# Loading v in the layout in which its products read it, and smaller edits around it

## The chip, the cores and the metric

The kernel runs on one core of a Trainium2 chip. The core has five engines with an instruction stream each: TensorE (PE) for matrix products into the accumulator memory (PSUM), VectorE (DVE), ScalarE (ACT) and GpSimd (POOL) for element-wise work, and SyncE (SP), which here only starts transfers. Sixteen DMA engines move data between the chip's memory and the core's working memory (SBUF, 128 partitions). The metric is the device time of one execution, in microseconds.

## The reference, cut to what matters

Two stages follow each other. The first is an attention without a softmax: each row of q and k (4 batches, 4 heads, 1088 tokens of 32 numbers) is sketched to two vectors of 8 numbers, and their outer product has 64 features. The second adds to the result the real part of its two-dimensional Fourier transform, normalizes each row and applies a small network of two layers.

```python
def phi(x):
    a = np.einsum('rd,bhsd->bhsr', S1, x)
    b = np.einsum('rd,bhsd->bhsr', S2, x)
    return np.einsum('bhsi,bhsj->bhsij', a, b).reshape(*x.shape[:-1], r * r)
q_p, k_p = (phi(q), phi(k))
kv = np.einsum('bhsf,bhsd->bhfd', k_p, v)
z = np.sum(k_p, axis=2)
num = np.einsum('bhsf,bhfd->bhsd', q_p, kv)
den = np.einsum('bhsf,bhf->bhs', q_p, z)[..., None] + 1e-06
x = num / den                        # then heads side by side: (4, 1088, 128)

X = np.fft.fft(np.fft.fft(x, axis=1), axis=2)
u = x + np.real(X)
un = (u - u.mean(-1)) / np.sqrt(u.var(-1) + 1e-06)
out = u + np.maximum(un @ w_ch1, 0.0) @ w_ch2
```

The sum z is a product with a column of ones, so the kernel appends ones to v and gets kv and z from one product.

## The kernel before, in words

The program is a list of named steps (`add` in `program`). Their order is written out by hand in `ORDER`, and with it the order of the instructions on each engine; each engine works its own list strictly in that order and waits where an input is not there yet. Where a step may run on several engines, `ENGINE` names one, else the first allowed is taken. `BANK` names the PSUM banks of each step, so a step also waits until the last reader of its bank is done. The token `11@0` in `ORDER` stands for eleven products of zeros into bank 0: they have no result and keep PE busy.

The batches are worked in the order 1, 0, 3, 2. The 1088 tokens of a head are 64 groups of 17. For one batch:

- **Loads** (SP): `ld_k`, `ld_v`, `ld_q`, each one transfer of 544 KB to 128 partitions. The tiles k_in, v_in and q_in have three buffers each, so the fourth batch's load waits until the third buffer has been read. The order on SP is k1, k0, q0, v1, q1, k3, v0, q3, w1, v2, w2, k2, v3, q2.
- **Features of k**: `kT` (DVE) transposes k in blocks of 32, `kproj` (PE) multiplies it by the sketches for all four heads at once (`sblk`), `kab` (ACT or DVE) copies the result out of PSUM, and four `kp` steps (POOL or DVE) form the outer products. The 16 tokens of a group that fill whole tiles take this way; `kproj` puts token 2t + h of each group in tile t, partitions 64 h and up. The seventeenth token has its own steps: `kt_pr`, `kt_a`, `kt_p`.
- **v**: `vcopy` (steps `vc`, on ACT or POOL) brings v into that token order and next to a column of ones (tile `v`, 33 of 36 columns), `vlast` (`vl`) does so for the seventeenth token (tile `vt`). The ones are written once (`c_v1`, `c_vt`).
- **Sums**: `kv` (PE, L396) multiplies the outer products by v and its ones, 33 columns, over 8 tiles and the seventeenth token (`kvt`); `kvz` copies the sums to where the next product reads them.
- **Features of q**: `qT`, `qt_T` (DVE transposes), `qfeat` (PE), `qa` (ACT copy out of PSUM), `qp` (DVE product); `pnd` (PE, L496) multiplies them by the sums, `den` and `xx` (DVE) divide.
- **Transform and network**: foldings of x by POOL and DVE, `srow` (PE), copies `zev`, `zrev`, `zleft` (steps `z`, `zr`, `zl`), then ten mixer units with `mix` or, for the seventeenth tokens of two batches, `mixl` (PE), row statistics, a transpose, the two layers, the copy `fin` and the store.

The start of the program also computes tables of sines and cosines (`t_` and `d_` steps) and constants (`c_` steps, mostly on POOL). The sketches S1 and S2 arrive by ACT's transfers `ld_s` and are transposed by PE in `s_t`; `s_blk` (DVE) makes `sblk` of it.

PE writes each 32-bit product as two records, so that the 36 products of `kv` per batch are 72 records.

## Time and profile before

| | |
|---|---|
| median of 3 runs | 82.59 us (82.38 to 83.35) |
| profiled execution | 82.68 us, of which span 80.9 us |
| PE, DVE busy | 70.3 us (87%), 65.8 us (81%) |
| ACT, POOL busy | 57.3 us (71%), 48.5 us (60%) |
| DMA queue of SP | 5332 packets, 9.31 MB |
| granted TensorE clock | 0.978 |

The span runs from the first to the last instruction of the profiled execution; the other 1.8 us of its time lie around it. Busy time is what an engine spent in instructions that compute; a share near one says that the engine is full, not that it is what the others wait for. The rows of a timeline give start and length in microseconds, engine, line, operation, output and inputs with their shapes, the number of instructions merged into the row, and in brackets how long the engine stood idle before it and who released it. Rows of busy times by stage give the stretch, its length, then busy time and count of PE, PE's weight loads, DVE, ACT and POOL, the granted clock, the share of time in which the DMA engines were busy, and GB/s.

### The profile page before, as it was taken

How to read it: one execution, taken by the hardware profiler on the slowest of the kernel's cores; microseconds unless marked ns; L12 is line 12 of the kernel's file. 1: busy time of each engine (PE TensorE's matmuls, PEld its weight loads, DVE VectorE, ACT ScalarE, POOL GpSimd, SP SyncE). 2: the span in 40 equal slices, each digit the busy share in tenths (PEclk: the TensorE clock that was granted, in tenths of full speed). 3: DMA queues.
4: the chain of work that ended last, by engine and by line, in shares of the span. 5: the costliest groups of instructions: out<-in, count | busy, mean ns of one | idle time of the engine just before them, and what ended most of it. 6: DMA issues, size and time to landing. Idle time of an engine off the chain costs nothing.

```text
span 80.9 us, 3298 instructions
## 1 busy us (share of the span) xinstructions
PE 70.3 (87%) x1380; PEld 51.7 (64%) x1385; DVE 65.8 (81%) x142; ACT 57.3 (71%) x106; POOL 48.5 (60%) x130
## 2 busy tenths in 40 slices
PE   4999997999999999999697999979999898999000
PEld 1326944969799887559576795655866793578000
DVE  2999839999989999999998959997987799867300
ACT  1447679999999996858619686785779889695100
POOL 6898699999799996879999990952400000000000
PEclk9999999999999999999999999999999999999965
DMA  1899999970360700000000000000035440404450
GB/s 23 300 424 409 420 420 392 373 263 23 39 245 17 271 0 4 8 0 0 8 0 8 0 0 0 8 0 0 0 91 169 128 139 12 135 15 138 116 161 14
DMA packets 5570, 9.65 MB, mean 119 GB/s; under 512 B 564, under 2 KB 3380, under 8 KB 5556
## 3 DMA queue, kind: packets, MB, share of 16 engines
q1 hardware_dynamic: 5332, 9.31, 33.4%
q8 instruction: 11, 0.18, 0.9%
q10 hardware_dynamic: 224, 0.14, 0.6%
q14 instruction: 3, 0.02, 0.1%
HBM read 7.22 MB, written 2.23 MB: 117 GB/s over the span
## 4 chain that ended last, share of the span: by engine, by line
PE 50%; POOL 24%; DVE 8%; ACT 7%; issue 3%; DVEq 1%; POOLq 0%; ACTq 0%
PE ps L496 8%; PE ps L673 7%; PE ps L396 7%; PE ps L651 6%; PE ps L444 6%; POOL t_kp__129 L79 4%; POOL t_kp__132 L79 3%; PE ps L560 3%; POOL t_kp__133 L79 3%; PE ps L591 2%; PE ps L643 2%; DVE t_x__147 L506 2%; PE ps L566 2%; POOL t_ph L185 2%; POOL t_e__149 L79 2%
## 5 line engine op out<-in xcount | busy, mean ns | idle before, releaser
L813 PE MATMUL ps<-t_wz 128*128 128x512 bf16 x19 | 6.8, 519 | 1.3 <-DVE t_eps L127 1.2
L72 ACT COPY t_qa__139<-ps 128x1024 f32<-128x1024 f32 x4 | 4.0, 1012 | 2.8 <-PE ps L444 2.8
L666 ACT ACTIVATE t_ht__112<-ps 128x1024 bf16<-128x1024 f32 x4 | 4.1, 1024 | 2.0 <-PE ps L651 1.8
L813 PEld LDWEIGHTS <-t_wz 128*128 128x128 bf16 x20 | 2.2, 121 | 4.7 <-issue 2.9
L651 PEld LDWEIGHTS <-t_w1b 128*128 128x128 bf16 x40 | 3.3, 97 | 3.0 <-issue 1.3
L72 ACT COPY t_qa__138<-ps 128x1024 f32<-128x1024 f32 x4 | 4.0, 1009 | 1.5 <-PE ps L444 1.5
L666 ACT ACTIVATE t_ht__111<-ps 128x1024 bf16<-128x1024 f32 (+1 forms) x4 | 3.5, 910 | 0.9 <-PE ps L651 0.7
L666 ACT ACTIVATE t_ht__113<-ps 128x1024 bf16<-128x1024 f32 x4 | 4.0, 1021 | 0.1
L651 PE MATMUL ps<-t_unT__178,t_w1b 128*128 128x512 bf16 (+1 forms) x14 | 3.4, 333 | 0.4 <-DVE t_x__147 L506 0.2
L651 PE MATMUL ps<-t_unT__180,t_w1b 128*128 128x512 bf16 x11 | 3.3, 378 | 0.4 <-ACT t_ht__112 L666 0.2
L454 DVE TENSOR_TENSOR t_qp__141<-ps,t_qa__139 128x1024 f32<-128x1024 f32 x2 | 2.5, 1225 | 1.4 <-ACT t_qa__139 L72 1.2
L496 PE MATMUL ps<-t_kvz,t_qp__140 128*64 128x66 f32 x96 | 3.4, 223 | 0.0
L496 PE MATMUL ps<-t_kvz,t_qp__141 128*64 128x66 f32 x96 | 3.4, 223 | 0.0
L496 PEld LDWEIGHTS ps<-t_kvz,t_qp__140 128*64 128x64 f32 x96 | 3.1, 138 | 0.4 <-ACT t_kvz L72 0.4
L496 PEld LDWEIGHTS ps<-t_kvz,t_qp__141 128*64 128x64 f32 x96 | 3.1, 138 | 0.0
L444 PE MATMUL ps<-t_qT__125,t_sa 32*64 32x256 f32 x64 | 2.9, 400 | 0.0
L444 PE MATMUL ps<-t_qT__126,t_sa 32*64 32x256 f32 x64 | 2.9, 400 | 0.0
L196 ACT ACTIVATE t_pm<-t_ph 128x290 f32<-128x290 f32 x3 | 1.3, 441 | 2.1 <-DVE t_ph L190 2.1
L668 DVE TENSOR_SCALAR t_ht__114<-ps 128x1024 bf16<-128x1024 f32 x2 | 2.4, 1221 | 0.4 <-PE ps L651 0.4
L79 POOL TENSOR_TENSOR t_kp__129<-t_ab__128 128x256 f32<-128x256 f32 x4 | 2.4, 628 | 0.5 <-issue 0.5
L444 PE MATMUL ps<-t_qT__126,t_sb 32*64 32x256 f32 x64 | 2.7, 374 | 0.0
L444 PE MATMUL ps<-t_qT__125,t_sb 32*64 32x256 f32 x64 | 2.7, 374 | 0.0
(338 smaller groups left out, 263.0 us busy)
## 6 DMA issues: line engine op xcount, KB each, us to landing
t_k_in__101<-in_k_dram SPq DMA_DIRECT2D x2, 544.0 KB, 6.4
t_q_in__107<-in_q_dram SPq DMA_DIRECT2D x2, 544.0 KB, 3.3
t_v_in__104<-in_v_dram SPq DMA_DIRECT2D x2, 544.0 KB, 7.4
out_dram<-t_ot__110 SPq DMA_DIRECT2D x6, 128.0 KB, 3.1
out_dram<-t_ot__108 SPq DMA_DIRECT2D x6, 128.0 KB, 2.3
t_k_in__100<-in_k_dram SPq DMA_DIRECT2D x1, 544.0 KB
t_k_in__99<-in_k_dram SPq DMA_DIRECT2D x1, 544.0 KB, 4.8
t_q_in__105<-in_q_dram SPq DMA_DIRECT2D x1, 544.0 KB, 5.6
```

Of the source, the lines that this page charges most:

```text
L72: nc.scalar.copy(out, in_)
L79: (nc.vector if e == "DVE" else nc.gpsimd).tensor_tensor(out=out, in0=in0, in1=in1, op=op)
L396: nc.tensor.matmul(ps(f"kv{b}", 33 * (h // 2), [[1, 33]], 64 * (h % 2), 64), w, v, start=(b, h % 2) not in begun, stop=True, tile_position ...
L444: nc.tensor.matmul(ps(f"q{b}.{w}", 512 * h + 256 * f, [[1, 256]], 64 * v, 64), view(T(src), 0, [[1, F]], 32 * h, 32), view(T(f"qT{b % 2}") ...
L454: nc.vector.tensor_tensor(out=view(T(f"qp{(2 * b + w) % 3}"), 127 * w, [[256, 4], [128, 2], [1 - 2 * w, 128]]), in0=ps(f"q{b}.{w}", 256, [ ...
L496: nc.tensor.matmul(ps(f"nd{b}", 512 * (i // 6) + 66 * (i % 6), [[1, 66]], 64 * h, 64), q, z, start=True, stop=True, tile_position=(0, 64 * ...
L560: nc.tensor.matmul(o, w, row(c, t, trig), start=(t == 0), stop=(t == 2), tile_position=(0, p), skip_group_check=True)
L651: nc.tensor.matmul(ps(use, 128 * n * i, [[1, 128 * n]]), T("w1b")[:, 128 * c:128 * c + 128], T(f"unT{g % 3}")[:, 0:128 * n], start=True, s ...
L666: nc.scalar.activation(out=out, in_=in_, func=ACT.Relu)
L668: nc.vector.tensor_relu(out, in_)
L673: nc.tensor.matmul(ps(u, 128 * t, [[1, 128]]), ht_view(g, 512 * c + 128 * t, [[1, 128]]), T("w2b")[:, c, :], start=False, stop=True, skip_ ...
L813: nc.tensor.matmul(made["ps"][:, at, :], made["wz"][:, 0:128], made["wz"][:], start=True, stop=True)
```

## The change

- `ld_v` loads v as two transfers of 64 partitions, one for each half y: partition 64 y + p gets, for each of the four heads, tokens 8 y to 8 y + 8 of group p, nine rows of 32 numbers in one piece. Token 8 is loaded twice, token 16 lies in the upper half only. v_in has four buffers, and behind the loaded rows each holds 32 ones, written once by `c_v1`.
- `vcopy`, `vlast`, the tiles `v` and `vt`, and `c_vt` are gone. `kv` reads v_in directly, 32 columns of v and the 32 ones as 64 columns; `kvz` reads the first 33 of each 64.
- `kproj` puts token t + 8 h, instead of 2t + h, in tile t, so that the outer products meet v in that order. The seventeenth token's features stand in partitions 64 to 127 for all four heads: `kt_pr` is one product of 64 columns instead of two of 32, and `kt_a` and `kt_p` work on 64 partitions with twice the columns.
- `mixl` adds x by one product with the identity `idb` per batch instead of two with `idl`, whose step `c_idl` is gone; `zleft` writes zl with gaps, so that the last rows come out in natural order, and `st_last` stores 128 rows of equal distance. `c_fz` clears the whole of zl.
- In `ORDER` the zero products around the transpose of the sketches become 13 ahead of it and 1 behind, from 11 and 5. All other steps keep their order.

```diff
     def ld_v(b):
-        nc.sync.dma_start(view(T(f"v_in{min(b, 2)}"), 0, [[TT * D, 2], [1, TT * D]]),
-                          dram(x["v"], b * H * S * D, [[TT * D, 128], [2 * S * D, 2], [1, TT * D]]))
+        for y in range(2):
+            nc.sync.dma_start(view(T(f"v_in{b}"), 0, [[9 * D, H], [1, 9 * D]], 64 * y, 64),
+                              dram(x["v"], (b * H * S + 8 * y) * D, [[TT * D, 64], [S * D, H], [1, 9 * D]]))
...
-        nc.gpsimd.memset(view(T("zl"), 16, [[48, 2 * B], [1, 16]]), 0.0)
+        nc.gpsimd.memset(T("zl")[:], 0.0)
...
+        add(f"c_v1{b}", "POOL DVE", "", f"v1:{b}", lambda e, b=b: (nc.gpsimd if e == "POOL" else nc.vector).memset(T(f"v_in{b}")[:, ONES:ONES + D], 1.0))
...
-                                 view(T(f"kT{b % 2}"), 64 * (2 * t + h), [[1, 64]]),
+                                 view(T(f"kT{b % 2}"), 64 * (t + 8 * h), [[1, 64]]),
...
     def kt_pr(b):
-        for u in range(2):
-            nc.tensor.matmul(ps(f"kt{b}", 0, [[1, 32]], 64 * u, 64), view(T(f"kT{b % 2}"), 64 * (TT - 1), [[1, 64]]),
-                             view(T("sblk"), 16 * u, [[32, 2], [1, 16]]), start=True, stop=True,
-                             tile_position=(0, 64 * u), skip_group_check=True)
+        nc.tensor.matmul(ps(f"kt{b}", 0, [[1, 64]], 64, 64), view(T(f"kT{b % 2}"), 64 * (TT - 1), [[1, 64]]), T("sblk")[:],
+                         start=True, stop=True, tile_position=(0, 64), skip_group_check=True)
...
-    def vcopy(b, y, e):
-
-        for u in range(2):
-            copy(e, view(T(f"v{b % 3}"), VP * u, [[2 * VP, 2], [VP * H, 8], [1, D]], 64 * y, 64),
-                 view(T(f"v_in{min(b, 2)}"), D * y, [[TT * D, 2], [2 * D, 8], [1, D]], 64 * u, 64))
-
-    def vlast(b, e):
-        copy(e, view(T("vt"), 2 * VP * b, [[VP, 2], [1, D]]), view(T(f"v_in{min(b, 2)}"), (TT - 1) * D, [[TT * D, 2], [1, D]]))
...
-                nc.tensor.matmul(ps(f"kv{b}", 33 * (h // 2), [[1, 33]], 64 * (h % 2), 64), w, v,
-                                 start=(b, h % 2) not in begun, stop=True, tile_position=at, skip_group_check=True)
+                nc.tensor.matmul(ps(f"kv{b}", 64 * (h // 2), [[1, 64]], 64 * (h % 2), 64), w,
+                                 view(T(f"v_in{b}"), at, [[ONES - at, 2], [1, D]], p, n),
+                                 start=(b, h % 2) not in begun, stop=True, tile_position=(p, 64 * (h % 2)), skip_group_check=True)
...
     def mixl(i):
         u = f"u{i}.2"
         for b in (2 * i, 2 * i + 1):
-            for par in range(2):
-                p, to = 64 * (b % 2), 64 * par + 32 * (b % 2)
-                nc.tensor.matmul(ps(u, 0, [[1, 128]], to, 32), view(T("idl"), 32 * par, [[1, 32]], p, 64),
-                                 view(T(f"x{b}"), 8 * DM, [[1, DM]], p, 64),
-                                 start=True, stop=False, tile_position=(p, to), skip_group_check=True)
+            p = 64 * (b % 2)
+            nc.tensor.matmul(ps(u, 0, [[1, 128]], p, 64), T("idb")[p:p + 64, p:p + 64], view(T(f"x{b}"), 8 * DM, [[1, DM]], p, 64),
+                             start=True, stop=False, tile_position=(p, p), skip_group_check=True)
...
-c_wz c_bias c_iota c_rows ld_k1.0 t_turn0 c_last c_kvz1 t_ph0 c_mask c_fwd c_v12 c_kvz2 ld_s c_vt c_eye16 kT1.0 11@0
-s_t s_blk 5@1 kt_pr1 ld_k0.0 c_v11 t_turn1 kT0.0 t_pm0 kpr1 t_cos0 s_ab t_sin0 kab1 kt_a1 ld_q0.0 c_tab kpr0 kab0
+c_wz c_bias c_iota c_rows ld_k1.0 t_turn0 c_last c_kvz1 t_ph0 c_mask c_fwd c_v12 c_v13 c_kvz2 ld_s c_eye16 kT1.0 13@0
+s_t s_blk 1@1 kt_pr1 ld_k0.0 c_v11 t_turn1 kT0.0 t_pm0 kpr1 t_cos0 s_ab t_sin0 kab1 kt_a1 ld_q0.0 c_tab kpr0 kab0
```

## The prediction

> **What bounds the kernel now.** I read the page's busy times first, then the engines by stage, then the timelines of TensorE (PE) and VectorE (DVE), then the loads. The page:

> ```profile
> span 80.9 us, 3298 instructions
> PE 70.3 (87%) x1380; PEld 51.7 (64%) x1385; DVE 65.8 (81%) x142; ACT 57.3 (71%) x106; POOL 48.5 (60%) x130
> ```

> No engine is idle for long, so the answer lies in stages. The busy times by stage:

> ```profile
> core 0: us, PE busy (x) PEld busy (x) DVE busy (x) ACT busy (x) POOL busy (x), PEclk, DMA share, GB/s
> 18.10:39.30 21.20, 21.20 (x604) 17.93 (x604) 20.05 (x35) 18.54 (x39) 18.87 (x49) 1.00 0.19 59
> ```

> From 18.1 to 39.3 us PE has no gap at all and DVE is busy for 20.05 of 21.2 us. The copies of v are on ACT and POOL; in this stage they are bystanders unless PE or DVE wait for them. The chain of work hands the time before 18.1 us to POOL:

> ```profile
> 16.45 1.67 POOL t_kp__129 L79 x2
> 18.11 2.86 PE ps L396 x88
> ```

> That reading is coarse: the first L396 products after 18.1 us read other tiles, and t_kp__129 comes last of batch 0's. So I go by the timelines. DVE:

> ```profile
> 11.76 1.23 DVE L454 TENSOR_TENSOR t_qp__141<-ps,t_qa__139 128x1024 f32<-128x1024 f32 x1 [1.24 <-ACT t_qa__139 L72]
> ...
> 14.80 0.25 DVE L368 TENSOR_TENSOR t_ktp__123<-ps,t_kta__121 128x128 f32<-128x128 f32 x1
> 15.21 1.22 DVE L454 TENSOR_TENSOR t_qp__140<-ps,t_qa__138 128x1024 f32<-128x1024 f32 x1 [0.15 <-ACT t_qa__138 L72]
> 16.35 0.23 DVE L461 STREAM_TRANSPOSE t_qtT__116<-t_q_in__107 128x64 f32<-128x64 f32 x1
> ...
> 17.54 0.41 DVE L472 TENSOR_TENSOR t_qtp<-ps,t_qta__117 128x256 f32<-128x256 f32 x1
> ...
> 20.75 1.30 DVE L358 STREAM_TRANSPOSE t_kT__119<-t_k_in__101 128x1088 f32<-128x1088 f32 x1
> 22.25 0.71 DVE L437 STREAM_TRANSPOSE t_qT__126<-t_q_in__107 128x512 f32<-128x512 f32 x1 [0.19 <-PE ps L444]
> 23.36 1.23 DVE L454 TENSOR_TENSOR t_qp__140<-ps,t_qa__139 128x1024 f32<-128x1024 f32 x1 [0.40 <-ACT t_qa__139 L72]
> ...
> 25.73 1.36 DVE L506 TENSOR_TENSOR t_x__145<-ps,t_den__143 128x1152 bf16<-128x1152 f32 x1
> ```

> DVE's rests between 11.76 and 24 us are 0.15, 0.19 and 0.40 us. It works strictly in the written order, so a load that lands late stops everything behind it. The third batch's load of k (t_k_in__101, second use) is read at 20.75 us, the fourth batch's q (t_q_in__107) at 16.35 us. When do loads land? SP's timeline (start, length of the issue), the DMA issues and the tile view:

> ```profile
> 2.12 0.44 SPq L100 DMA_DIRECT2D t_v_in__103<-in_v_dram  x1
> 2.60 0.47 SPq L109 DMA_DIRECT2D t_q_in__106<-in_q_dram  x1
> 3.12 0.53 SPq L93 DMA_DIRECT2D t_k_in__101<-in_k_dram  x1
> ...
> 7.27 0.38 SPq L119 DMA_DIRECT2D t_w2f<-in_moe_w_ch_dram  x1
> 14.91 0.34 SPq L93 DMA_DIRECT2D t_k_in__101<-in_k_dram  x1
> ```

> ```profile
> t_v_in__103<-in_v_dram SPq DMA_DIRECT2D x1, 544.0 KB, 6.5
> t_q_in__106<-in_q_dram SPq DMA_DIRECT2D x1, 544.0 KB, 7.4
> ...
> t_w2f<-in_moe_w_ch_dram SPq DMA_DIRECT2D x1, 256.0 KB, 10.5
> ```

> ```profile
> DMA to landing us min/median/max: 4.6/6.4/8.2
> ```

> (The last is t_k_in__101: 8.2 is the use of 3.12, in a full queue, 4.6 that of 14.91.) So v1 lands at 8.6 us, q1 at 10.0, k3 at 11.3: one 544-KB load in about 1.35 us. Continued at that pace v0 is there at 12.7, q3 at 14.0, w1 at 14.6, v2 at 16.0, w2 at 16.6 (measured 7.27 + 10.5 = 17.8) and k2, issued at 14.91, at 19.5 as measured. Needed at 16.35 and 20.75: q3 has 2.3 us to spare, k2 1.25 us. That is the number that the change can spend.

> **The loads of v.** The new ld_v issues two transfers per batch, each to 64 of the 128 partitions, in pieces of 9 x 32 x 4 = 1152 bytes; together 2 x 64 x 4 x 1152 B = 590 KB instead of 557 KB (544 KB in the page's unit). v1, v0 and v2 stand ahead of k2. What did the rate hang on so far? The busy times of three stretches (last column GB/s):

> ```profile
> 6.90:8.40 1.50, 1.50 (x41) 1.16 (x40) 1.50 (x5) 0.79 (x2) 1.22 (x5) 1.00 1.08 431
> 8.40:9.90 1.50, 1.50 (x56) 1.43 (x60) 1.27 (x6) 1.07 (x3) 1.01 (x8) 1.00 1.01 418
> 15.25:16.00 0.75, 0.75 (x32) 0.75 (x31) 0.75 (x1) 0.73 (x2) 0.75 (x3) 1.00 1.35 377
> ```

> By the order of the queue these are mostly v1 (2176-byte pieces), q1 (4352) and w2 (512): 431, 418, 377 GB/s. Piece length hardly counts, so 1152 bytes cost next to nothing: 590 KB at 418 is 1.41 us, +0.08 per load. What no row varies is the partitions: every one of these transfers reaches all 128. Hence two ends for a half-partition transfer: the full rate (+0.08 us a load), or, if the flat 418 is a sum over the partitions reached, half of it, 209 GB/s: 590 KB in 2.82 us, +1.49 a load. I take the half: the rate was the same for three piece lengths and three tensors, so it is set by what these have in common, and of that the change halves one thing. Both ends stay in the range.

> [...]

> At half rate the landings become: v1 10.1, q1 11.5, k3 12.8, v0 15.6, q3 17.0, w1 17.6, v2 20.4, w2 21.1, k2 22.4 by the pace; w2 was 1.2 us behind the pace before, so k2 lies in 22.4 to 23.6, and I take 22.7. Issuing does not limit this: in the listing of the changed program a load waits until the eighth one before it has landed, so w2 waits for q1 (11.5 us) and k2 for its buffer, each long before its turn. v3 no longer waits for a buffer and follows k2.

> **What the late loads cost.** q1 at 11.5 eats the gain at the start (below). q3 at 17.0 holds DVE's L461 by 0.6 us, and with it L472 (17.54), which frees the PSUM banks of batch 0's sums; the PE starts them about 0.5 us later. Then k2: the transpose of 20.75 starts at 22.7, +1.95. Behind it on DVE wait the transposes of q, L454 of 23.36 (which PE's products L496 for batch 1 read), the divisions and x (25.73). The rests of 0.19 and 0.40 absorb 0.59: +1.36 for x0. From there to the first row transform:

> ```profile
> 25.73:35.50 9.77, 9.77 (x249) 7.39 (x252) 9.40 (x17) 7.95 (x16) 8.58 (x20) 1.00 0.18 61
> ```

> DVE is busy 9.40 of 9.77 us. The 0.37 us may take up a little more, which the range covers; I count nothing. PE, full before, reads what DVE writes and is behind by the same.

> **The copies.** Each batch loses four wide copies (64x512) and a narrow one; two batches' wide ones on ACT, and what stood between them:

> ```profile
> 11.75 2.52 ACT L72 COPY t_v__136<-t_v_in__103 64x512 f32<-64x512 f32 x4
> 14.18 1.00 ACT L72 COPY t_qa__138<-ps 128x1024 f32<-128x1024 f32 x1
> 15.47 2.52 ACT L72 COPY t_v__135<-t_v_in__102 64x512 f32<-64x512 f32 x4
> ```

> The first four hold up t_qa__138 by at most 14.18 - 11.75 = 2.4 us. But its reader on DVE waited only 0.15 us for it (15.21); before it DVE has its own work. The 0.40 us at 23.36 would be the only other gain, and k2's wait takes its place. POOL's copies are worth nothing: what POOL does late, it does because of others:

> ```profile
> 36.16 0.36 POOL L76 COPY t_zl<-t_z__160 128x32 bf16<-128x32 bf16 x2 [0.48 <-ACT t_z__160 L72]
> ```

> POOL waits there for ACT's copy of PE's row transform, and only then makes the last products of k for batch 2. With PE and DVE as they are, no copy of v stands ahead of that.

> **Zero products.** 16 become 14 around the sketches, 13 ahead and 1 behind. PE's weight loads and first sums:

> ```profile
> 5.89 0.13 PEld L325 LDWEIGHTS ps<-t_id,t_s 16*128 16x128 f32 x1 [0.74 <-POOL t_ph L186]
> 6.05 0.76 PEld L813 LDWEIGHTS <-t_wz 128*128 128x128 bf16 x5
> 7.24 0.20 PEld L363 LDWEIGHTS ps<-t_sblk,t_kT__120 128*64 128x64 f32 x4 [0.42 <-issue]
> ```

> Five behind take 7.24 - 6.05 = 1.19 us, 0.22 each once PE runs quickly. Two more ahead put the transpose at 6.3; one behind lets L363 start at about 6.8 after the mask product on DVE: -0.45 us. It goes through L454 (11.76), which ACT feeds, as long as q1's small transpose is not late: at half rate it is: q1 at 11.5 and 0.2 us for the transpose, against 11.76 - 0.45 = 11.3. What is left, 0.1 us, the wait for k2 swallows.

> **Products and small things.** The sums with v read 64 columns instead of 33. The PE timeline and the chain:

> ```profile
> 18.45 0.66 PE L396 MATMUL ps<-t_v__135,t_kp__130 128*64 128x33 f32 x16
> ...
> 20.34 0.64 PE L396 MATMUL ps<-t_v__136,t_kp__134 128*64 128x33 f32 x16
> ```

> ```profile
> 24.32 0.98 PE ps L346 x32
> 26.23 0.09 PE ps L363 x4
> ...
> 70.04 0.17 PE ps L606 x4
> ```

> 64 records in 20.34 - 18.45 = 1.89 us are 29.5 ns each; L346, whose form is 128*64 128x64, takes 30.6. For 288 records (36 products a batch, two records each): +0.3 us on a full PE; at half rate PE waits for DVE and hides half of that. L363 loses half its records, -0.05 a batch, which cancels the other half. kt_p goes from 128x128 (0.25) to 64x256; the nearest row is L472 with 256 columns, 0.41: +0.13 on DVE per batch, two of them behind kT2, +0.26. L606 becomes two products: -0.06 for each of two uses. The store of the last rows has the same bytes, the cleared zl is larger but its stage waits for others on POOL, c_idl stood ahead of a rest of POOL: 0.

> **Sum** against the profiled execution (82.68 us, span 80.9): +1.36 + 0.26 - 0.12 (L606) = +1.5, 84.2. The median of the runs is 82.59, so 84.1.

> **Rivals.** (1) *Full-rate halves*, 0.30: k2 at 19.6, no stall. -0.45 at the start, +0.3 for 64 columns, +0.1 for kt_p, -0.2 for L363 and L606: -0.25, 82.3, within 81.7 and 82.8; not slower. For it: sixteen DMA engines moved 377 GB/s even of 512-byte pieces. Against it: nothing here reaches half the partitions. It decides below about +0.9 us per v load: k2 is then at 22.7 - 3 x (1.49 - 0.9) = 20.9, and the transpose, due at 20.75 - 0.45 = 20.3, is late by no more than the rests of 0.59. (2) *The whole delay is passed on*, 0.08: k2 at 24.0 (19.5 + 3 x 1.49): +2.6, 85.2. (3) *ACT was the bound*, 0.05: if the 2.4 us of t_qa__138 reached PE, 82.59 - 0.45 - 2.4 = 79.7; the 0.15 us of 15.21 speaks against it. (4) *64 columns cost in proportion*: 288 x 29.5 x 31/33 ns = 8 us; L346 excludes it, 0.02.

> **How the numbers follow.** Half rate or near it has 0.55, from 83.2 (k2 at 21.8) to 85.0 (k2 at 23.6, the late end of the landings above). The range 82.0 to 85.0 leaves out (2), (3), (4) and the low end of (1). Two per cent, what a measurement here can tell from no change, is 80.9 and 84.2: somewhat under half of the half-rate case lies above it, with (2) and (4) 0.36; below it is (3), 0.05; 0.59 between.

> **What would show it.** Right: the stretch of v1 moves some 210 GB/s, k2 lands after 22 us, DVE stands still for over 1 us before kT of batch 2, and x0 ends about 28.5 instead of 27.1 us. Wrong: landings as before, L358 at 20.3 us and x0 before 27 us; or a PE gap at L396, which would mean that v itself came late; or L396 records well above 31 ns.

## The result and the profile after

| | before | after |
|---|---|---|
| median of 4 runs each | 82.61 us (82.38 to 83.35) | 85.84 us (85.60 to 86.03) |
| ratio, 95% interval | | 1.037 (1.030 to 1.045) |
| span of the profiled execution | 80.9 us | 84.1 us |

Ratios, here and below, use the faster executions of each kernel alone, medians use all of them, and five of the profiles below (halves in the kernel before, k2 first, v3 held, the half-partition backlog, the second run with natural last rows) are of slower executions.

The change made the kernel 3.7% slower. The forecast was 84.1 us, with 82.0 to 85.0 as its range: the sign was right, the size wrong, and the time lies outside the range.

The page of the kernel after, its span and busy times:

```profile
span 84.1 us, 3249 instructions
PE 71.7 (85%) x1366; PEld 51.9 (62%) x1371; DVE 66.3 (79%) x142; ACT 50.2 (60%) x93; POOL 45.0 (54%) x120
```

ACT lost 7.1 us of busy time and POOL 3.5, and yet the span is 3.2 us longer. The busy times by stage (last column GB/s) show the loads. The first row is a load of q, to all partitions; the other three lie in the loads of v1, v0 and v2:

```profile
5.30:6.60 1.30, 1.30 (x4) 0.29 (x2) 0.95 (x1) 1.28 (x2) 1.18 (x3) 1.00 1.01 416
7.00:8.50 1.50, 1.50 (x36) 1.20 (x35) 1.38 (x3) 0.69 (x2) 1.19 (x6) 1.00 1.10 243
12.50:14.00 1.50, 1.06 (x30) 0.57 (x18) 1.47 (x3) 0.89 (x1) 1.50 (x4) 1.00 1.15 239
17.50:19.00 1.50, 1.24 (x37) 0.71 (x33) 0.20 (x2) 0.09 (x1) 1.43 (x12) 1.00 1.09 227
```

VectorE's timeline, at the places that the prediction named (L438 is the small transpose of q, L461 before; L349 that of k, L358 before; L483 the division, L506 before):

```profile
18.80 0.25 DVE L438 STREAM_TRANSPOSE t_qtT__115<-t_q_in__106 128x64 f32<-128x64 f32 x1 [1.58 <-DMA t_q_in__106<-in_q_dram]
...
19.54 0.41 DVE L449 TENSOR_TENSOR t_qtp<-ps,t_qta__116 128x256 f32<-128x256 f32 x1
...
26.34 1.31 DVE L349 STREAM_TRANSPOSE t_kT__118<-t_k_in__99 128x1088 f32<-128x1088 f32 x1 [3.63 <-DMA t_k_in__99<-in_k_dram]
...
30.50 1.36 DVE L483 TENSOR_TENSOR t_x__141<-ps,t_den__139 128x1152 bf16<-128x1152 f32 x1
```

DVE stood still for 1.58 us for q3 and for 3.63 us for k2. And TensorE's timeline, where L375 are the sums with v:

```profile
20.00 0.45 PE L375 MATMUL ps<-t_v_in__100,t_ktp__122 64*64 64x64 f32 x8 [1.27 <-DVE t_qtp L449]
...
21.83 0.40 PE L375 MATMUL ps<-t_v_in__100,t_kp__128 128*64 128x64 f32 x6
24.65 0.51 PE L375 MATMUL ps<-t_v_in__100,t_kp__128 128*64 128x64 f32 x10 [2.42 <-issue]
24.94 0.69 PE L375 MATMUL ps<-t_v_in__101,t_kp__133 128*64 128x64 f32 x16
```

PE starts the sums of batch 0 at 20.00 us instead of 18.10, since L449 holds a bank that they need, and then stops for 2.42 us in the middle of one group of 16 records that read the same tiles. "issue" says that no event in the profile released it. The same sums of batch 1 start at 24.94 instead of 20.34 us (+4.60), x0 at 30.50 instead of 25.73 (+4.77).

At the end of the program something came back. The last copies of the two kernels run at 75.46 and 80.53 us (+5.07), but the spans differ by 3.2. These are the last copy, the last store's issue and a stretch of its transfer, before:

```profile
75.46 0.28 DVE L74 COPY t_ot__108<-ps 128x128 f32<-128x128 f32 x1
...
76.83 0.54 SPq L688 DMA_DIRECT2D out_dram<-t_ot__108  x1
...
78.50:79.00 0.50, 0.00 (x0) 0.00 (x0) 0.00 (x0) 0.00 (x0) 0.00 (x0) 0.50 0.15 44
```

and after:

```profile
80.53 0.28 DVE L74 COPY t_ot__107<-ps 128x128 f32<-128x128 f32 x1
...
81.27 0.54 SPq L662 DMA_DIRECT2D out_dram<-t_ot__107  x1
...
82.00:82.50 0.50, 0.00 (x0) 0.00 (x0) 0.00 (x0) 0.00 (x0) 0.00 (x0) 0.50 0.99 324
```

44 GB/s at a share of 0.15 of the 16 engines against 324 at 0.99. From the end of the last copy to the end of the span it is 80.9 - 75.74 = 5.16 us before and 84.1 - 80.81 = 3.29 after: 1.87 us won. So the change is +5.07 up to the last copy, -1.87 behind it, +3.2 in sum.

### The profile page after: what moved, and what is told of

Read it like the earlier page. It is cut to its first block, busy times and chain, and to the rows that moved or that the text cites. A ratio compares the mean times of both kernels' runs of the same rounds, so it can differ in the third digit from the quotient of the medians.

```text
span 84.1 us, 3249 instructions
## 1 busy us (share of the span) xinstructions
PE 71.7 (85%) x1366; PEld 51.9 (62%) x1371; DVE 66.3 (79%) x142; ACT 50.2 (60%) x93; POOL 45.0 (54%) x120
## 2 busy tenths in 40 slices
DMA packets 6685, 9.77 MB, mean 116 GB/s; under 512 B 656, under 2 KB 5520, under 8 KB 6672
## 4 chain that ended last, share of the span: by engine, by line
PE 49%; DMA 20%; DVE 8%; ACT 7%; POOL 5%; issue 4%; ACTq 1%; SPq 1%; DVEq 1%
DMA t_q_in__106<-in_q_dram 15%; PE ps L473 8%; PE ps L375 7%; PE ps L647 7%; PE ps L625 6%; PE ps L421 5%; DMA t_s<-in_S_dram 5%; PE ps L537 3%; PE ps L568 2%; PE ps L617 2%; POOL t_kp__131 L79 2%; DVE t_x__143 L483 2%; PE ps L543 2%; POOL t_e__145 L79 2%; PE ps L563 1%
## 5 line engine op out<-in xcount | busy, mean ns | idle before, releaser
L72 ACT COPY t_qa__134<-ps 128x1024 f32<-128x1024 f32 x4 | 4.1, 1013 | 6.3 <-PE ps L421 6.3
L72 ACT COPY t_qa__135<-ps 128x1024 f32<-128x1024 f32 x4 | 4.1, 1014 | 4.7 <-PE ps L421 4.7
L79 POOL TENSOR_TENSOR t_kp__128<-t_ab__127 128x256 f32<-128x256 f32 x4 | 2.4, 626 | 6.0 <-PE ps L375 6.0
L72 ACT COPY t_kvz<-ps 64x66 f32<-64x66 f32 x12 | 2.5, 211 | 4.9 <-PE ps L375 4.8
L640 ACT ACTIVATE t_ht__111<-ps 128x1024 bf16<-128x1024 f32 x4 | 4.1, 1024 | 2.0 <-PE ps L625 1.8
L349 DVE STREAM_TRANSPOSE t_kT__118<-t_k_in__99 128x1088 f32<-128x1088 f32 x1 | 1.3, 1315 | 3.6 <-DMA t_k_in__99<-in_k_dram 3.6
L375 PE MATMUL ps<-t_v_in__100,t_kp__128 128*64 128x64 f32 x16 | 0.9, 224 | 2.4 <-issue 2.4
L421 PE MATMUL ps<-t_qT__125,t_sb 32*64 32x256 f32 x64 | 2.7, 374 | 0.0
## 6 DMA issues: line engine op xcount, KB each, us to landing
t_k_in__99<-in_k_dram SPq DMA_DIRECT2D x2, 544.0 KB
t_q_in__106<-in_q_dram SPq DMA_DIRECT2D x2, 544.0 KB, 7.9
t_v_in__102<-in_v_dram SPq DMA_DIRECT2D x2, 288.0 KB, 12.7
```

The costliest lines, as they stand in the source:

```text
L72: nc.scalar.copy(out, in_)
L79: (nc.vector if e == "DVE" else nc.gpsimd).tensor_tensor(out=out, in0=in0, in1=in1, op=op)
L375: nc.tensor.matmul(ps(f"kv{b}", 64 * (h // 2), [[1, 64]], 64 * (h % 2), 64), w, view(T(f"v_in{b}"), at, [[ONES - at, 2], [1, D]], p, n), s ...
L421: nc.tensor.matmul(ps(f"q{b}.{w}", 512 * h + 256 * f, [[1, 256]], 64 * v, 64), view(T(src), 0, [[1, F]], 32 * h, 32), view(T(f"qT{b % 2}") ...
L640: nc.scalar.activation(out=out, in_=in_, func=ACT.Relu)
```

## The experiments

**Loads of v to all partitions, the rest as after.** The theory was that half the partitions make a transfer slow; its rival that pieces, bytes and the number of transfers do.

```diff
-            nc.sync.dma_start(view(T(f"v_in{b}"), 0, [[9 * D, H], [1, 9 * D]], 64 * y, 64),
-                              dram(x["v"], (b * H * S + 8 * y) * D, [[TT * D, 64], [S * D, H], [1, 9 * D]]))
+            nc.sync.dma_start(view(T(f"v_in{b}"), 18 * D * y, [[9 * D, 2], [1, 9 * D]]),
+                              dram(x["v"], (b * H + 2 * y) * S * D, [[8 * D, 128], [S * D, 2], [1, 9 * D]]))
```

> The kernel after, but each of the two transfers of v reaches all 128 partitions and brings two heads instead of reaching 64 partitions with four heads; bytes (590 KB a batch), pieces (1152 B) and the number of transfers stay. Partition p gets the nine rows from 8 p on, so other rows of v than the reference wants are summed. Theory A (what costs is that a transfer reaches half the partitions): v moves at 400 GB/s or more, k2 lands before 21 us, DVE's waits of 1.58 us for q3 and 3.63 us for k2 and PE's 2.42 us in the sums of batch 0 go, and the 5.1 us that the chain lost by then come back: 80.7 us (80.2 to 81.6). Theory B (the shorter pieces, the 6% more bytes and the two transfers for one are what costs): 85 to 86 us as after.

Measured: 81.87 us, ratio to before 0.985 (0.980 to 0.990), span 79.1. The stretches of v1 and v0, and DVE's wait that is gone:

```profile
6.70:8.10 1.40, 1.40 (x46) 1.31 (x44) 1.40 (x4) 1.38 (x4) 1.25 (x5) 1.00 1.10 396
10.80:12.10 1.30, 1.23 (x33) 0.71 (x32) 0.91 (x1) 0.35 (x1) 1.30 (x3) 1.00 1.12 398
```

```profile
16.23 0.23 DVE L438 STREAM_TRANSPOSE t_qtT__115<-t_q_in__106 128x64 f32<-128x64 f32 x1
```

x0 starts at 25.50, PE has no stop. The whole loss hangs on the halves: between this kernel and the kernel after there is nothing else but which rows of v are read, and it is 4.0 us by the medians. The median is 0.3 us above the range that the theory gave, and the rival's 85 to 86 us are far off.

**The halves alone, in the kernel before.**

```diff
-        nc.sync.dma_start(view(T(f"v_in{min(b, 2)}"), 0, [[TT * D, 2], [1, TT * D]]),
-                          dram(x["v"], b * H * S * D, [[TT * D, 128], [2 * S * D, 2], [1, TT * D]]))
+        for y in range(2):
+            nc.sync.dma_start(view(T(f"v_in{min(b, 2)}"), 0, [[TT * D, 2], [1, TT * D]], 64 * y, 64),
+                              dram(x["v"], (b * H + y) * S * D, [[TT * D, 64], [2 * S * D, 2], [1, TT * D]]))
```

> The kernel before with one edit: each load of v is two transfers of 64 partitions, same bytes, same pieces of 2176 B, same layout. Theory A: each v load takes 2.67 us (557 KB at 209 GB/s) instead of 1.33, three of them ahead of k2: k2 lands 4 us later than 19.5 or more, and the time rises by 2.5 to 5 us, to 85.1 to 87.6 us (the copies are late as well). Theory B: one more transfer a load, within 0.5 us of 82.6.

Measured: 88.47 us, ratio 1.063 (1.054 to 1.072), more than either theory gave. DVE waits 1.4 us for q3 and 1.5 for k2, and PE stops here too:

```profile
21.03 0.22 PE L397 MATMUL ps<-t_v__135,t_kp__129 128*64 128x33 f32 x1
23.37 0.85 PE L397 MATMUL ps<-t_v__135,t_kp__129 128*64 128x33 f32 x12 [2.12 <-issue]
```

So the halves alone make it, with the old pieces and the old layout. Part of the excess can lie in PE's granted clock, which is 0.50 from 23 to 28 us, behind the stop; what that costs was not measured. The stop was the new thing to explain.

**What is PE's stop?** The theory: PE's own instructions arrive through the same 16 engines, and behind a backlog of loads a piece of the program comes late. Then the stop must fall at the same instruction number, whatever the time and the work. The busy times by stage up to the stop count PE's products and weight loads. After, and the kernel before with halves:

```profile
0.00:22.50 22.50, 18.96 (x348) 12.07 (x350) 17.75 (x43) 9.14 (x13) 16.93 (x63) 1.00 0.97 283
```

```profile
0.00:21.20 21.20, 18.25 (x350) 11.82 (x350) 16.70 (x42) 14.07 (x22) 16.70 (x55) 1.00 0.96 284
```

698 and 700 instructions, in two programs with different layouts, at 22.5 and 21.2 us. Two runs move the backlog. The first changes the order of the loads:

```diff
-ld_w1 ld_v2 ld_w2 kt_p0 ld_k2.0 ...
+ld_w1 kt_p0 ld_k2.0 ...
...
-... ld_v3 qT3.0 ...
+... ld_v2 ld_w2 ld_v3 qT3.0 ...
```

> The kernel after with the loads v2 and w2 issued behind k2 instead of ahead of it (order ... q3, w1, k2, v2, w2, v3, q2); v2 is first read by the sums of batch 2, long after. Both theories: k2 lands before 20.5 us, and DVE's wait of 3.63 us for it goes; the one for q3 (1.58 us) stays. Theory A (PE's stop of 2.42 us in the sums of batch 0 is a fetch of its own instructions, held up by the half-partition transfers that are queued until 24 us): the backlog still lasts to about 24 us, so the stop stays, after the same number of PE instructions (348 products and 350 weight loads) with 1.5 us or more, and little is won: 84.3 to 85.6 us. Theory B (k2's landing alone makes the kernel late, the stop is beside it or a consequence of it): 82.3 to 83.3 us.

Measured: 85.56 us, ratio 1.030 (1.019 to 1.040), in theory A's range. k2's wait is gone, q3's is 1.81 us, and PE stops later:

```profile
28.03 0.28 PE L473 MATMUL ps<-t_kvz,t_qp__137 128*64 128x66 f32 x2 [1.28 <-issue]
...
0.00:26.90 26.90, 22.95 (x477) 15.71 (x478) 21.22 (x47) 12.59 (x25) 20.70 (x70) 1.00 0.94 254
...
32.68 0.22 PEld L421 LDWEIGHTS ps<-t_qT__125,t_sa 32*64 32x64 f32 x6 [0.55 <-issue]
...
0.00:32.60 32.60, 27.50 (x605) 19.67 (x605) 25.42 (x55) 15.34 (x30) 24.45 (x77) 1.00 0.83 228
```

The expectation was wrong on the place: not after 698 instructions but after 477 + 478 = 955, and a second one after 605 + 605 = 1210. The distances are 955 - 699 = 256 and 1210 - 955 = 255. The second run held v3 back:

```diff
-            nc.sync.dma_start(view(T(f"v_in{b}"), 0, ...
+            nc.sync.dma_start(view(T(f"v_in{(0, 1, 2, 1)[b]}"), 0, ...
```

> The kernel after with three buffers of v instead of four: v3 takes the buffer of v1 and can be issued only when the sums of batch 1 have read it (after 22 us); all other loads as in after. Theory A (v3's two transfers right behind k2 share the engines with k2's last pieces and keep the backlog up): k2 lands about 2 us earlier, at 23.5 to 24.5 us instead of 26.3, PE's stop ends by 23 us, and the time is 83.0 to 84.8 us. Theory B (k2 is late by what stands ahead of it, v3 doesn't matter): k2 lands at 26 us, 85.4 to 86.2 us.

Measured: 86.40 us, ratio 1.037 (1.026 to 1.047): theory A, that v3 behind k2 makes k2 late, falls. No stop in PE, but DVE waits 2.84 us for q3 and then 1.65 for k2, which is read from 25.92 us although nothing stands behind it. Most of k2 moves in the first of these two stretches, its last pieces in the second and after it:

```profile
22.00:23.00 1.00, 1.00 (x22) 1.00 (x22) 1.00 (x3) 0.00 (x0) 0.00 (x0) 0.50 1.03 379
23.00:24.00 1.00, 1.00 (x24) 1.00 (x22) 1.00 (x2) 0.00 (x0) 0.00 (x0) 0.50 0.38 101
```

379 GB/s is near the pace of the loads to all partitions here (396 to 416 GB/s in the stretches above). Then the share of time in which the DMA engines are busy falls to 0.38, and DVE still waits: the last pieces are what it waits for.

**A backlog without halves of v.** The kernel before with natural last rows (below), and five loads behind k2 that nobody reads, to all partitions in one run and to the lower 64 in the other:

```diff
+    for i in range(5):
+        add(f"ld_x{i}", "SP", "", f"xx:{i}", ...)   # 1024 columns of 128 (or 64) partitions of a tile not in use yet
...
-... ld_k2.0 ...
+... ld_k2.0 ld_x0 ld_x1 ld_x2 ld_x3 ld_x4 ...
```

> The kernel before with the last rows in natural order (81.2 us), and five more loads of 524 KB to all 128 partitions behind k2, into tiles that are not in use yet; nobody reads them. They keep the 16 engines busy from about 18 to 24.5 us, and nothing that is needed by then stands behind them. Theory A (PE fetches its instructions through the same engines, and any backlog holds the fetch up): PE stops after some 700 recorded instructions (350 products, 350 weight loads) or 256 later, for 1 us or more, 82.3 to 84.0 us. Theory B (only transfers to half the partitions hold it up): no stop, 80.9 to 81.7 us.

> The same with the five loads on partitions 0 to 63 alone (262 KB each), which at some 210 GB/s keep the engines busy just as long. Theories A and B: PE stops after some 700 recorded instructions or 256 later, for 1 to 2.5 us, 82.3 to 84.0 us. If it doesn't stop, the stops have nothing to do with transfers to half the partitions, and 80.9 to 81.7 us come out.

Measured: 84.71 us (83.03 to 85.96, no ratio on record) and 85.20 us, ratio of the second 1.028 (1.020 to 1.036); the same kernel without the five loads has 81.22. The profiled execution of the first took 83.03 us, in theory A's range; both medians lie above the ranges. Both stop, the first (to all partitions) here:

```profile
24.81 0.39 PE L493 MATMUL ps<-t_kvz,t_qp__141 128*64 128x66 f32 x6 [1.10 <-issue]
...
0.00:23.60 23.60, 21.21 (x477) 15.23 (x478) 19.75 (x46) 17.90 (x33) 21.35 (x71) 1.00 0.94 361
```

the second here:

```profile
27.87 0.39 PE L493 MATMUL ps<-t_kvz,t_qp__141 128*64 128x66 f32 x6 [3.72 <-issue]
...
0.00:26.00 26.00, 21.94 (x477) 15.42 (x478) 21.39 (x47) 19.88 (x38) 23.56 (x76) 1.00 0.95 300
```

955 instructions again. In the first run no engine waits for a load by then (the second reads k2 0.46 us late); what is late there, if theory A holds, is PE's program. From 27 us on the five also delay v3, for which POOL waits 0.99 us in the first run and 3.60 in the second. Theory A's stop is there, 1.10 us long, so a backlog of full loads does it too. How far halves do it more can't be read from one profile each.

The traces hold more on this than the counts. The page's list of DMA queues has two of the kind "instruction", q8 and q14; the larger one in the kernel after:

```profile
q8 instruction: 10, 0.16, 0.9%
```

These are ten transfers of 16 KB. In the kernel before, the second of them begins at 15.99 us and ends at 17.32, and PE reaches its 700th recorded instruction at 19.9: nothing stops. In the kernel after it begins at 21.90 and ends at 23.33; PE, which has stood since 22.23, goes on at 24.65. The same holds for every stop of 0.4 us or more behind a backlog, nine in seven profiles: PE goes on 1.3 to 1.5 us after the end of a transfer of q8. In the run with v3 held it is as late (22.22 to 23.28), but PE reaches its 700th instruction only at 24.8, and doesn't stop. That these transfers carry PE's instructions is not named in the trace; it rests on this match.

**Which partitions, or how many?** The two transfers of v go to every second partition:

```diff
+            a = T(f"v_in{b}")[:]
+            step = a.ap[0][0]
+            nc.sync.dma_start(bass.AP(tensor=a.tensor, offset=a.offset + y * step, ap=[[2 * step, 64], [9 * D, H], [1, 9 * D]]), ...
...
-        nc.vector.transpose(view(T(f"kT{b % 2}"), 64 * lo, [[1, 2], [64, n], [2, 32]]), ...
+        nc.vector.transpose(view(T(f"kT{b % 2}"), 0, [[2, 2], [1, 2], [128, 9], [4, 32]]), ...
...
+            nc.tensor.matmul(ps(f"k{b}", 64 * t, [[1, 64]]), view(T(f"kT{b % 2}"), 128 * t, [[1, 128]]), T("sblk")[:], ...
```

> The kernel after with the two halves of v on every second partition: the transfer for y goes to the 64 partitions 2 p + y, the same rows, bytes and pieces as after. The transpose of k writes its columns in that order (18 blocks instead of 17, +0.08 us each on DVE), L337 is one product of 128 columns instead of two of 64, and the last token's features are multiplied by 0 in the even partitions. Theory A1 (the rate hangs on which partitions are reached: 0 to 63 or 64 to 127 is one side, every second one is all of them): v moves at 400 GB/s or more, no waits for q3 and k2, no stop of PE, 80.4 to 82.2 us. Theory A2 (the rate hangs on how many partitions are reached, 64 either way): v at 210 to 250 GB/s and the waits of after, 85 to 86.5 us.

Measured: 86.22 us, ratio 1.045 (1.038 to 1.051). The rates are near A1's, the time isn't:

```profile
6.70:8.10 1.40, 0.79 (x7) 0.80 (x8) 1.40 (x3) 0.98 (x3) 1.18 (x6) 1.00 1.10 389
11.00:12.50 1.50, 1.50 (x36) 1.05 (x37) 0.99 (x4) 0.58 (x1) 1.50 (x4) 1.00 1.11 373
```

```profile
L339 PE MATMUL ps<-t_sblk,t_kT__119 128*128 128x64 f32 x32 | 4.0, 278 | 0.0
...
L350 DVE STREAM_TRANSPOSE t_kT__119<-t_k_in__100 128x1152 f32<-128x1152 f32 x1 | 2.4, 2359 | 0.0
```

With 64 partitions spread over the memory, v moves at 373 to 389 GB/s, against 396 and 398 for all 128 in the first experiment; no wait for q3 or k2, no stop. So the rate hung on which partitions a transfer reached, not on how many: the lower and upper halves moved 227 to 243 GB/s in the kernel after, 0.55 to 0.58 of the 416 of a load to all. The time was lost elsewhere, in two things that I had put at next to nothing: the transpose takes 2.36 us instead of 1.31 when its output goes in steps of 16 bytes instead of 8 (with one dimension more in its pattern), and a product with 128 weight columns 4.0 / 32 = 0.125 us a record, where in the kernel after one with 64 columns takes 2.5 / 64 = 0.04. That these make up the 4.4 us to the first experiment was not tried alone.

**Natural order of v.** One transfer of 128 partitions with tokens 8 m to 8 m + 7, the transpose writing tokens in order:

```diff
+        nc.sync.dma_start(view(T(f"v_in{b}"), 0, [[8 * D, H], [1, 8 * D]]), dram(x["v"], b * H * S * D, [[8 * D, 128], [S * D, H], [1, 8 * D]]))
...
+            nc.tensor.matmul(ps(f"k{b}", 64 * t, [[1, 64]]), view(T(f"kT{b % 2}"), t, [[8, 128]]), T("sblk")[:], ...
```

> The kernel after with another layout of v that reaches all 128 partitions with one transfer: partition m gets tokens 8 m to 8 m + 7 of the four heads (524 KB in pieces of 1024 B), and a second transfer brings the last 64 tokens of the four heads (33 KB); the transpose of k writes its tokens in natural order, so that one product of 128 columns per tile, with a stride of 8 through kT, takes the place of two of 64 (16 records of L337 instead of 32 per batch). Theory A: loads as before, no stops, and half of L337's records less, 0.5 us a batch of a full PE, of which the part in the stage before 39 us counts: 80.2 to 81.4 us. Theory B (DVE, not PE, sets that stage): as the run with full-partition transfers, 81.5 to 82.3 us.

> The run with the natural layout of v, with the zero products of before (11 ahead of the transpose of the sketches and 5 behind it) instead of 13 and 1. Theory A (all of them run at 0.43 us each on a PE that is not yet quick): the transpose of the sketches at about 6.0 instead of 6.9 us, the first product with the sketches 0.1 to 0.3 us earlier, the time 0.1 to 0.4 us less. Theory B (the prediction's: 13 and 1 start the products 0.45 us earlier): 0.2 to 0.5 us more.

Measured: 98.87 us, ratio 1.190 (1.181 to 1.199), and 97.43 us (95.52 to 99.44). Both theories missed it by 17 us:

```profile
L337 PE MATMUL ps<-t_sblk,t_kT__119 128*128 128x64 f32 x32 | 8.2, 420 | 0.1
```

8.2 us for two batches: 0.26 us a record with weights in steps of 32 bytes, 4.1 us a batch, against 2.5 us for 64 records, 1.25 a batch, in the kernel after. The granted clock is low as well: 0.50 from 9.7 to 19.9 us and 0.51 from 26.7 to 33.6, while PE is busy throughout. How the 17 us divide between the two was not tried. The pair says nothing on the zero products: the transpose of the sketches started at 6.02 instead of 6.59 us, the first product behind it at 7.34 instead of 7.26.

**The upper halves on ACT's queue**, beside SP's loads:

```diff
+        add(f"lu_v{b}", "ACT", "", f"v_in:{b}/1", lambda e, b=b: ld_v(b, e, 1))
...
-... t_pm0 kpr1 ... t_sin0 kab1 ... qT0.1 ld_v1 ... ld_v3 ...
+... t_pm0 lu_v1 kpr1 ... t_sin0 lu_v0 kab1 ... lu_v2 qT0.1 ld_v1 ... ld_v3 lu_v3 ...
```

> The kernel after with the upper half of each v load issued by ACT (behind t_pm0, t_sin0 and ahead of qT0.1's place in the order, so that it runs beside SP's full loads) instead of by SP behind the lower half. Bytes, pieces and partitions of each transfer stay. Theory A (the partitions of one half are a port that is full while the other stands idle; a half transfer beside others is no loss): the 16 engines together move 350 GB/s or more until the backlog is gone, which is by 20 us instead of 24, q3 lands by 17.5 us and k2 by 22, 81.0 to 83.5 us. Theory B (each half transfer is slow by itself, whatever runs beside it, and holds the engines): the backlog lasts to 23 us or more, 84.5 to 86.5 us.

Measured: 89.12 us, ratio 1.076 (1.066 to 1.085). The engines move 269 to 342 GB/s between 6 and 18 us, and the backlog lasts past 22 us; but this doesn't decide between the theories, because ACT itself was stopped:

```profile
14.20 0.60 ACTq L100 DMA_DIRECT2D t_v_in__102<-in_v_dram  x1
14.84 1.01 ACT L72 COPY t_qa__135<-ps 128x1024 f32<-128x1024 f32 x1 [4.51 <-DMA t_k_in__99<-in_k_dram]
```

The issue of a load waited for an earlier load, and ACT's copies behind it. PE then stood for 4.62 us, and stopped again after 698 and after 1209 instructions.

**The store of the last rows.** In the kernel after, the old pattern; in the kernel before, natural order of the last rows (`zleft`, `mixl`, `c_fz`, `st_last` as after, no `idl`):

```diff
-        nc.sync.dma_start(dram(x["out"], 2 * i * S * DM, [[17 * DM, 128], [1, DM]]), ot(g)[:, 0:128])
+        nc.sync.dma_start(dram(x["out"], 2 * i * S * DM, [[17 * DM, 2], [34 * DM, 64], [1, DM]]), ot(g)[:, 0:128])
```

> The kernel after with the store of the last rows in the DRAM pattern of before (two sets of 64 rows); it writes the rows of the last tokens to each other's places. Theory A: the last store moves at some 45 GB/s instead of 240 or more, and the end of the span is 1.3 to 1.9 us later: 87.1 to 87.7 us. Theory B: the gain at the end is from the products or from SP's order, not from the pattern: 85.8.

> The kernel before with the last rows in natural order alone: zl with gaps, one product of x per batch with the identity, no idl, the store of 128 equal distances. Theory A (the store to rows of two interleaved sets is what took long at the end): the tail from the end of the chain of products to the end of the span falls from 5.2 to about 3.3 us, 80.7 us (80.3 to 81.2). Theory B (the prediction's, same bytes: nothing): 82.4 to 82.8.

Measured: 87.82 us, ratio 1.063 (1.057 to 1.070), and 81.22 us, ratio 0.982 (0.976 to 0.989). The old pattern in the kernel after:

```profile
83.00:84.00 1.00, 0.00 (x0) 0.00 (x0) 0.00 (x0) 0.00 (x0) 0.00 (x0) 0.58 0.14 44
```

Both lie just above theory A's ranges. The pattern is worth 2.0 us by the medians of the one, and the last rows as a whole 1.6 by those of the other. The profiles give the pattern less: with the old one the kernel after ends 4.64 us behind its last copy instead of 3.29, so 1.35 of the 1.87 us. The other 0.5 goes with SP, which issues the last store 0.46 us behind the last copy in the kernel after, with either pattern, and 1.09 behind it in the kernel before; why it is later there was not tried. With two interleaved sets of rows the 16 engines are busy for 0.14 of the time here and 0.15 in the kernel before, with one even set for 0.99; why the old pattern keeps them so idle, no run shows.

**The zero products**, on a kernel whose loads are in time:

```diff
-... kT1.0 11@0
-s_t s_blk 5@1 kt_pr1 ...
+... kT1.0 13@0
+s_t s_blk 1@1 kt_pr1 ...
```

> The kernel before with the last rows in natural order, and with 13 zero products ahead of the transpose of the sketches and 1 behind instead of 11 and 5. Theory A (the zero products run at 0.43 us each until PE is quick, and when that is differs from one execution to the next): the median within 0.3 us of the same kernel with 11 and 5, beside it; the transpose of the sketches starts anywhere from 5.9 to 6.9 us. Theory B (the prediction's: -0.45 us, not swallowed here since the loads are in time): 0.3 to 0.5 us less.

> The kernel before with the last rows in natural order, on the same chip as the run with 13 and 1 zero products, as its mate. Both theories: 80.9 to 81.6 us.

Measured: 81.38 us, ratio 0.979 (0.974 to 0.984), and 81.70 us, ratio 0.981 (0.976 to 0.986). 0.2% apart, within the intervals: theory A's bound of 0.3 us is just missed by the medians (0.32 apart) and met by the ratios, and whether the step is worth anything isn't settled. Why it can go either way, the start of PE in the kernel after shows:

```profile
1.19 5.73 PE L787 MATMUL ps<-t_wz 128*128 128x512 bf16 x13 [1.19 <-DVE t_eps L128]
6.85 0.23 PE L316 MATMUL ps<-t_id,t_s 16*128 16x16 f32 x1
```

and in the first experiment, which has the same instructions there:

```profile
1.19 4.46 PE L787 MATMUL ps<-t_wz 128*128 128x512 bf16 x13 [1.19 <-DVE t_eps L128]
5.85 0.20 PE L316 MATMUL ps<-t_id,t_s 16*128 16x16 f32 x1 [0.21 <-DMA t_s<-in_S_dram]
```

Thirteen products take 5.73 us in one execution and 4.46 in the other. When PE becomes quick differs from one to the next.

Of the kernels here, the kernel before with natural last rows beats both kernels, and with 13 and 1 zero products it is no worse.

## Why the prediction was right or wrong

- **Half rate of the loads of v: right here**, in kind and nearly in size (227 to 243 GB/s against 209). The reason given, that the rate is a sum over the partitions reached, is not: every second partition moves at 373 to 389 GB/s with as many of them. The first rival, full-rate halves, would have been true for that choice of 64.
- **The landings: the step that failed.** "At half rate the landings become ... q3 17.0 ... k2 22.7": they were read at 18.80 and 26.34. The pace counts a load as landed when its bytes have gone by at 1.35 us a load. What a reader waits for is the last piece, and behind halves that comes late. The counts of DMA packets show it for k2, 128 pieces of 4352 bytes, in the stretches 19.50 to 22.10, 22.10 to 24.00 and 24.00 to 26.30 us of the kernel after; no other load there has pieces over 2 KB, so the last number less the one before it counts k2's:

```profile
DMA packets 589, 0.84 MB, mean 323 GB/s; under 512 B 30, under 2 KB 469, under 8 KB 587
DMA packets 382, 0.42 MB, mean 222 GB/s; under 512 B 22, under 2 KB 375, under 8 KB 382
DMA packets 93, 0.12 MB, mean 51 GB/s; under 512 B 13, under 2 KB 89, under 8 KB 92
```

118 pieces begin before 22.1 us, about where the pace has k2's landing, and the other ten from 22.9 to 25.0 us. In the kernel before, the last ten begin within 0.9 us. A load behind halves also begins slowly: the stretches in which q1 and q3 begin, and one behind the first of them, with q1 and k3 almost alone:

```profile
9.00:10.50 1.50, 1.50 (x60) 1.34 (x54) 1.40 (x4) 1.05 (x3) 1.15 (x5) 1.00 1.00 320
14.30:15.90 1.60, 1.60 (x52) 1.53 (x53) 1.57 (x2) 0.37 (x1) 1.60 (x3) 1.00 0.97 321
10.00:12.00 2.00, 1.84 (x43) 0.95 (x36) 1.55 (x4) 1.36 (x2) 1.91 (x5) 1.00 1.01 412
```

320 and 321 GB/s, then 412, the full pace again. Why the last pieces come so late, no run shows.
- **"w2 waits for q1, v3 follows k2": no matter.** Held back, v3 changed nothing in the time (ratio 1.037 in both).
- **What the late loads cost: +1.36 predicted, 4.77 measured at x0.** The path is the one described, DVE's wait for k2: its transpose starts 5.59 us later instead of 1.95, 0.82 of that is absorbed, and from there to x0 DVE has no rest. q3's wait of 1.58 us, behind a later start, put the sums of batch 0 back by 1.9 us instead of 0.5, through L449 as described. The prediction knew nothing of PE's stop of 2.42 us. It lies beside the wait for k2: with the old store pattern, and the loads of the kernel after, the stop is 0.83 us and x0 still starts at 30.64 instead of 30.50. "A PE gap at L396 would mean that v itself came late" was wrong: v was there; what PE lacked was, by the match with q8, its program. Taking one of the two away doesn't bring the time back (k2 first, with stops: 85.56; v3 held, with no stop: 86.40); taking the backlog away does (81.87).
- **Copies of v as bystanders: right as far as seen.** Without them and with loads in time the ratio is 0.985, and the kernel before with nothing but the new last rows has 0.982 and 0.981: no net gain that can be measured. What their loss gives without the 64 columns and the larger `kt_p` was not tried.
- **64 columns, `kt_p`: fits.** A group of 16 records takes 0.64 us as before, `kt_p` takes 0.43 instead of 0.25, and from x0 to the last copy the delay grows from 4.77 to 5.07, 0.3 against the 0.26 predicted. That it is `kt_p` that makes the 0.3, no run shows alone.
- **Zero products: right by chance or wrong by chance.** "-0.45 us" took it that PE is quick by then. It was in the first experiment (L354 at 6.50 us instead of 7.24), it wasn't in the profiled execution of after (7.40).
- **"The store of the last rows has the same bytes: 0": wrong**, 1.35 of the 1.87 us won behind the last copy. The row that would have told it was there: the end of the profile before, 44 GB/s in the last transfer. I had looked at no stretch behind the last copy.
- **The sum**: +1.5 predicted, +5.07 - 1.87 = +3.2 measured. The rival that passes the whole delay on, 85.2 us at 0.08, was nearest, by luck: it has k2 at 24.0 instead of 26.3 and nothing for the store.

## What to carry to other kernels

A transfer was priced here by which partitions it reached (227 to 243 GB/s for 64 in one half, 373 to 389 for every second one) and by how the rows of a store lay (44 GB/s in two interleaved sets, up to 324 in one even set), before its bytes; and a load queued behind slow ones was there when its last piece was, which for k2 was 3.6 us after its pace said. A backlog of loads cost more than late data: TensorE stood for 0.40 to 3.72 us behind it, by the match with q8 for its own program, so look for an "issue" stop that falls on the same instruction number in several runs, and at when the transfers of the instruction queue end. Read the stretch behind the last copy too: it was 5.16 us of the span before and 3.29 after.
